# A written-out order of all steps, replaced by another: gated linear attention followed by a cosine-gated MLP

## The chip, the cores and the metric

The kernel runs on one core of one Trainium2 chip. The metric is the device time of one execution in microseconds; lower is better. Five engines work side by side, each through its own list of instructions in order: PE (TensorE, matmuls), ACT (ScalarE), DVE (VectorE), POOL (GpSimd), and SP (SyncE, which here only issues transfers).

## The reference

```python
# q, k, v, f_logit: 4 x 8 x 768 x 48 (batch, head, time, dim), float32
f = 1 / (1 + exp(-f_logit))
for t in range(768):
    state = f[:, :, t, :, None] * state + k_t (outer) v_t
    y[:, :, t] = q_t @ state
x = y as 3072 tokens x 384
h = x @ w_in                 # 384 -> 2048
out = (h * cos(h)) @ w_out   # 2048 -> 384
```

## The kernel before

The recurrence is computed in chunks. The 3072 tokens are twelve **pairs** `n` of two chunks (256 tokens), three pairs to a batch entry; within an entry the state goes from pair to pair. A pair is a set of named steps, most of them for the two halves `u` of the heads (suffix `.0`, `.1`):

- `f k q v` (SP, L309): loads. Pairs 0 and 1 fetch f, k and q by halves (192 KB each), everything else is 384 KB. `w0.i` and `w1.i` (L295, 768 KB) are the four parts of w_in and of w_out, `wc` their casts to bf16 (POOL or ACT, L196).
- `ex`, `ln` (ACT, L342, L346): softplus of the gate. `fx`, `fy`, `ka`, `qa`, `ad` (ACT and POOL, L350 to L373): the pairing of two neighbouring tokens in all pairs but 0 and 1.
- `cum` (PE, L386 and L392): running sums of the logarithms with the mask `incl`; `eb`, `ei` (ACT, L403, L407): their exponentials.
- `km`, `qm` (POOL, in pairs 0 and 1 also DVE, L416): k and q times those. `tk`, `tq` (PE, L451) transpose them in pairs 0 to 3 and `qkt` (L196) copies that out of PSUM; from pair 4 on `tq` is a transposing transfer on SP (L440).
- `sc` (PE, L472) scores, `am` (DVE, L494) their mask. `vb`, `vt` (POOL or ACT, L196) are copies of v.
- `ps` (PE, L512), `si` (PE, L529, pair 1 alone), `st`, `sz` (DVE, L538, L544): the state's sum, carry and decay.
- `y`, `yi` (PE, L572): the output inside the chunk and from the state; `xe` (ACT or DVE) copies it to bf16.

Behind a pair stands unit `m` of the MLP with the same 256 tokens: `h m.j s` (PE, L634, six matmuls, eight of these steps), `co` (ACT, cosine, L639), `g` (DVE, h times cosine, L616), and for each block of 128 tokens four steps `o` (PE, L650, four matmuls each), `ot` (copy) and `out` (store, L661). `z...` are memsets of padding (POOL or DVE, L241); `zf` (L277) is a matmul of zeros into a bank that nobody reads.

What runs when is one table, `ORDER`: every step once, with the letter of its engine (T PE, S ACT, V DVE, G POOL, Y SP) and the number of the buffer place that it takes. `emit` goes through it once and gives every engine its steps in this order; nothing is sorted afterwards. An instruction waits only for data, or for the place that its buffer frees.

Of the kernel before, what the change touches and what calls it, by code (L numbers as in the profile page):

```python
# [39 lines left out]
zsp.2:V zsz.0:V f1.0:Y ln1.1:S2 zvt.0:V zsp.1:V cum1.1:T2 k0.1:Y zf2:T3 q0.1:Y ei1.1:S0 vb0:G0  # L40
zf3:T1 ex0.1:S zf4:T4 f2:Y0 ex0.0:S vt0.2:G0 zf5:T6 ln0.0:S1 eb1.1:S0 cum0.0:T0 v1:Y1 ln0.1:S zf6:T5
zf7:T7 ei0.0:S1 zf8:T6 zf9:T6 cum0.1:T7 km0.0:G0 zf10:T4 f3:Y1 ei0.1:S zf11:T3 eb0.0:S1 zsz.3:G
tk0.0:T4 zf12:T6 eb0.1:S vt0.3:G km0.1:V ps0.0:T2,0 vt0.1:S k1.0:Y ex1.0:S ps0.1:T zf13:T6 sz0.00:V0
q1.1:Y0 vt0.0:S zf14:T6 zf15:T3 sz0.01:V zf16:T5 q1.0:Y st0.11:V zf17:T1 tk0.1:T6 ex2:S km1.1:V2
zf18:T1 w0.1:Y0 qm0.0:V tk1.1:T3 ln2:S1 zf19:T7 qm0.1:V tq0.0:T zf20:T5 vb1:S1 qkt0.0:V2 w0.0:Y3
ad2:G1 ln1.0:S sz0.11:V3 sc0.0:T4 tq0.1:T st0.10:V zsz.1:G ex3:S cum2:T2 am0.0:V1 w0.2:Y1 cum1.0:T7
vt1.1:G2 zf21:T1 ei1.0:S vt1.2:G zf22:T1 zf23:T1 ei2:S1 qkt0.1:V0 zf24:T4 km1.0:G zf25:T5 eb1.0:S
sz0.10:V ln3:S0 sc0.1:T6 ps1.1:T0,4 am0.1:V0 zf26:T1 eb2:S0 k3:Y2 ad3:G1 ps1.0:T fx3:S si1.0:T
tk1.0:T1 fx2:S qm1.0:V yi0:T5 qm1.1:G y0:T6 sz1.01:V1 tq1.0:T xe0.1:S2 cum3:T7 sz1.00:V w0.3:Y2
xe0.0:S qkt1.0:V0 tq1.1:T fy2:S zf27:T2 wc0.1:G qkt1.1:V1 eb3:S1 sc1.0:T0 ei3:S0 am1.0:V3 yi1:T3,2  # L50
vt1.0:S sc1.1:T6 q3:Y2 si1.1:T vt1.3:G am1.1:V0 h0.10:T0 wc0.0:S h0.11:T sz1.10:V1 sz1.11:V y1:T
w1.2:Y4 h0.01:T6 xe1.1:V0 wc0.2:G xe1.0:V h0.00:T co0.1:S3 k2:Y1 h1.01:T2 ka3:G h1.21:T4 fy3:S
g0.1:V0 co0.0:S2 h1.00:T km3.0:G2 h1.20:T w1.0:Y3 co1.0:S0 g0.0:V wc0.3:G h1.10:T0 co1.2:S3 h1.11:T
q2:Y1 g1.0:V1 qa3:G h0.30:T6 co1.1:S1 g1.2:V h0.31:T qm3.1:G h0.21:T2 co0.3:S2 g1.1:V km3.1:G
h0.20:T h1.31:T4 g0.3:V v3:Y2 qm3.0:G co0.2:S1 h1.30:T wc1.2:G tk3.0:T0 g0.2:V co1.3:S2 tq3.0:T
tq3.1:T6 w1.1:Y2 tk3.1:T qkt3.1:S2 ka2:G qkt3.0:V3 o2.2:T1 g1.3:V o1.2:T7 km2.1:G0 v2:Y1 o0.2:T0
wc1.0:S km2.0:G o3.2:T6 w1.3:Y4 sc3.0:T2 sc3.1:T4 qa2:G am3.0:V0 o0.0:T f4:Y2 o3.0:T qm2.1:G
am3.1:V2 vb3:S2 o2.0:T qm2.0:G tk2.1:T2 vt3.3:S0 tq2.1:T tk2.0:T3 qkt2.1:V4 f5:Y1 tq2.0:T ps3.0:T4,5
qkt2.0:V0 ps3.1:T wc1.1:G o1.0:T sz3.01:V0 sc2.0:T2 sz3.00:V k5:Y0 am2.0:V1 vb2:G0 o3.1:T o2.1:T
vt2.2:S2 vt3.1:G vt3.2:G ps2.1:T4 ps2.0:T sc2.1:T2 k4:Y2 st2.00:V wc1.3:G o0.1:T am2.1:V3 o1.1:T  # L60
st3.10:V v4:Y2 vt2.1:G o1.3:T ex4:S st3.11:V vt2.0:G o3.3:T ot1:V0 ln4:S1 vt2.3:G q4:Y1 o0.3:T
sz2.00:V3 ex5:S st2.01:V ad4:G2 o2.3:T sz2.01:V fx4:S ot3:V1 q5:Y2 ln5:S0 vt3.0:G cum4:T4 ot2:V2
y2:T2,3 ei4:S2 yi2:T ad5:G2 fy5:S yi3:T6 f9:Y0 y3:T1 xe2.0:V2 fx5:S ka4:G xe2.1:V fy4:S cum5:T7
sz3.10:V1 ei5:S0 h2.11:T2 sz3.11:V ka5:G out2:Y eb5:S2 xe3.1:V1 h2.10:T eb4:S0 xe3.0:V km4.1:G2
h2.21:T6 ot0:V3 v5:Y1 h2.01:T4 km4.0:G co2.1:S2 h2.00:T h3.21:T0 qa4:G co2.0:S3 g2.1:V1 h3.20:T
f6:Y2 qm4.0:G h2.20:T co3.2:S1 g2.0:V h2.31:T2 qm4.1:G co2.2:S0 h2.30:T g3.2:V3 vb4:G2 tq4.1:Y0
h3.11:T4 co2.3:S2 qa5:G g2.2:V h3.10:T h3.31:T0 vt4.2:S0 vt4.3:G f7:Y1 g2.3:V co3.1:S3 h3.30:T
vt4.0:G km5.1:G0 o5.1:T7 co3.3:S1 g3.1:V tq4.0:Y1 o4.0:T6 qm5.1:G o5.2:T g3.3:V q6:Y0 qm5.0:G
ps4.0:T4,5 sc4.1:T2 ps4.1:T o5.3:T st4.00:V ex6:S vb5:G0 tq5.1:Y4 st4.01:V o4.1:T sz4.01:V3 km5.0:G
ln6:S0 sz4.00:V o5.0:T out1:Y st4.11:V zsz.2:G fx6:S o6.3:T0 am4.1:V2 k6:Y2 ex7:S vt5.1:G2 o6.1:T  # L70
vt5.3:G tq5.0:Y3 ln7:S1 st4.10:V ps5.1:T1 ad6:G1 ps5.0:T sc4.0:T2 sz4.10:V2 o4.2:T am4.0:V3 fx7:S
zqk.1:G v6:Y2 o4.3:T vt4.1:S vt5.0:G ot5:S0 cum6:T4 sz4.11:V ad7:G2 ot4:S2 yi4:T2,3 st5.01:V ei6:S0
y4:T sz5.01:V1 eb6:S1 vt5.2:G sc5.1:T6 st5.00:V xe4.1:S2 xe4.0:V cum7:T5 o6.2:T out4:Y am5.1:V1
ka6:G ei7:S2 v7:Y0 eb7:S0 h4.00:T2 out3:Y km6.0:G0 sz5.00:V sc5.0:T4 k7:Y0 h4.01:T am5.0:V3 out0:Y
h3.00:T6 q7:Y1 co4.0:S2 vb6:G0 zvt.1:V y5:T1,4 km6.1:G yi5:T g4.0:V2 h3.01:T xe5.0:S3 fy6:S
ps6.1:T5,1 ps6.0:T xe5.1:S h4.31:T2 q8:Y2 qa6:G sz6.01:V3 co3.0:S2 sz6.00:V h4.30:T qm6.1:G h5.10:T4
g3.0:V co4.3:S3 h5.11:T vt6.1:G1 h4.21:T6 qm6.0:G g4.3:V co5.1:S0 h4.20:T ka7:G tq6.0:Y2 fy7:S
h4.10:T2 g5.1:V0 co4.2:S1 vb7:G2 h4.11:T k9:Y1 h5.21:T4 vt7.2:G0 g4.2:V co4.1:S2 h5.20:T km7.0:G1
tq6.1:Y4 o6.0:T vt6.2:S g4.1:V km7.1:G co5.2:S3 o9.2:T6 f8:Y2 vt6.0:G o9.3:T vt6.3:S g5.2:V qa7:G
# [693 lines left out]
```

## Time and profile before

| | us |
|---|---|
| three runs | 179.11, 179.11, 179.7; median 179.11 |
| the profiled execution, own time | 179.25 |
| its span on the core | 177.4 |
| DVE, ACT, POOL busy | 134.3, 128.9, 106.3 |

The span counts from the first recorded instruction to the last; 1.85 us of the execution's own time lie around it. Granted clock of TensorE over the span: 0.998. "Busy" means that at least one instruction of the engine was under way. In the views below "idle before" is how long the engine stood in front of an instruction, and the name behind the arrow is what ended it. Groups and timeline give first the line of the kernel, then the tile written and the tiles read.

### The profile page before, as it was taken

Reading aid. Unit: us, or ns where it says so; the run is one execution under the profiler, and the core shown is the slowest. Engines: PE = TensorE matmul, PEld = TensorE weight load, DVE = VectorE, ACT = ScalarE, POOL = GpSimd, SP = SyncE. Lnnn points to the kernel's source line nnn. Section 1 sums busy time; section 2 is a strip of 40 time slices with the busy share of each in tenths; the row PEclk is TensorE's granted clock in tenths of the full one; section 3 lists DMA queues with packets and bytes.
Section 4 is the critical chain, followed back from the end, with each engine's and each line's share of the span. In section 5 each row is a group of like instructions: output and inputs, shape, how many; then the busy total and the mean of one; then the engine's idle time right before and its main releaser. Section 6 shows DMA issues by size and latency. Waiting matters only on the chain.

```text
span 177.4 us, 5663 instructions
## 1 busy us (share of the span) xinstructions
PE 168.1 (95%) x2402; PEld 121.8 (69%) x2402; DVE 134.3 (76%) x201; ACT 128.9 (73%) x179; POOL 106.3 (60%) x134
## 2 busy tenths in 40 slices
...
GB/s 137 321 323 370 351 378 372 285 366 322 252 137 108 147 260 232 262 299 147 231 242 263 315 155 154 204 199 193 0 0 167 166 0 89 81 60 0 44 4 133
DMA packets 74394, 34.45 MB, mean 194 GB/s; under 512 B 67457, under 2 KB 72833, under 8 KB 74369
## 3 DMA queue, kind: packets, MB, share of 16 engines
...
q8 instruction: 19, 0.31, 0.8%
q14 instruction: 7, 0.05, 0.1%
...
## 4 chain that ended last, share of the span: by engine, by line
PE 85%; DVE 7%; POOL 3%; ACT 3%; issue 1%; POOLq 0%; DVEq 0%
PE ps L650 36%; PE ps L634 34%; PE ps L572 5%; PE ps L472 4%; PE ps L386 2%; PE ps L512 2%; DVE qk L416 2%; PE ps L451 1%; DVE qkt L196 1%; DVE incl L217 1%; ACT bj L403 1%; DVE sz L544 1%; PE ps L277 1%; DVE x L196 1%; DVE am L494 1%
## 5 line engine op out<-in xcount | busy, mean ns | idle before, releaser
L616 DVE TENSOR_TENSOR g<-ps,co 128x1024 bf16<-128x1024 f32 x48 | 57.8, 1222 | 15.4 <-ACT co L639 13.4
L650 PE MATMUL ps<-w_out_bf,g 128*128 128x384 bf16 x384 | 67.3, 326 | 0.0
L634 PE MATMUL ps<-x,w_in_bf 128*128 128x256 bf16 x576 | 66.3, 273 | 0.2 <-DVE x L196 0.2
L639 ACT ACTIVATE co<-ps,halfpi 128x1024 bf16<-128x1024 f32 x48 | 52.7, 1113 | 16.9 <-PE ps L634 13.0
L634 PEld LDWEIGHTS <-w_in_bf 128*128 128x128 bf16 x576 | 55.5, 98 | 8.5 <-issue 0.4
L650 PEld LDWEIGHTS <-g 128*128 128x128 bf16 x384 | 36.2, 98 | 22.4 <-DVE g L616 0.2
L494 DVE TENSOR_TENSOR am<-ps,pmask 128x1024 bf16<-128x1024 f32 x24 | 28.6, 1218 | 5.8 <-PE ps L472 4.5
L416 POOL TENSOR_TENSOR qk<-k,bi 128x384 bf16<-128x384 f32 x20 | 19.8, 1000 | 0.6
L416 POOL TENSOR_TENSOR qk<-q,b 128x384 bf16<-128x384 f32 x20 | 19.7, 999 | 0.7
L373 POOL TENSOR_TENSOR sp<-ls 128x384 bf16<-128x384 f32 x10 | 10.0, 998 | 13.3 <-ACT ls L346 7.1
L196 POOL COPY vt<-vb 64x384 bf16<-64x384 bf16 x32 | 16.0, 501 | 2.6 <-ACT vb L196 1.0
L196 ACT COPY ot<-ps 128x384 f32<-128x384 f32 (+1 forms) x10 | 4.5, 461 | 12.7 <-PE ps L650 6.9
L544 DVE TENSOR_TENSOR sz<-ps,b 64x192 bf16<-64x192 f32 x32 | 11.3, 354 | 1.3 <-PE ps L512 0.4
L196 DVE COPY ot<-ps 128x384 f32<-128x384 f32 (+1 forms) x16 | 8.1, 514 | 5.5 <-PE ps L650 5.5
L360 POOL TENSOR_TENSOR k<-k,f 128x384 f32<-128x384 f32 x10 | 10.0, 1002 | 3.4 <-ACT ot L196 3.3
L538 DVE TENSOR_TENSOR ps<-ps,sz 64x192 f32<-64x192 f32 x28 | 10.3, 366 | 1.8 <-PE ps L512 0.8
L342 ACT ACTIVATE f<-f 128x768 f32<-128x768 f32 (+1 forms) x14 | 10.3, 746 | 1.0 <-DMA f<-in_f_logit_dram 0.8
L277 PE MATMUL ps<-zero 128*128 128x512 bf16 x28 | 9.8, 445 | 1.2 <-DVE zero L203 1.2
L350 POOL TENSOR_TENSOR q<-f,q 128x384 f32<-128x384 f32 x10 | 10.0, 1000 | 1.3 <-ACT f L353 1.3
L196 ACT COPY vt<-vb 64x384 bf16<-64x384 bf16 x16 | 8.1, 508 | 2.4 <-POOL vb L196 2.1
L472 PE MATMUL ps<-qkt 48*64 48x128 bf16 (+1 forms) x320 | 8.8, 219 | 0.7 <-DVE qkt L196 0.6
L196 POOL CAST vb<-v 128x768 bf16<-128x768 f32 x8 | 6.6, 824 | 4.7 <-DMA v<-in_v_dram 3.4
...
## 6 DMA issues: line engine op xcount, KB each, us to landing
...
```

The source lines that it names most:

```text
L196: (nc.scalar.copy if e == "ACT" else eng(e).tensor_copy)(out=o, in_=i)
L277: G.step(f"zf{i}", ("PE",), lambda e, dump=dump: nc.tensor.matmul(dump.ap, lhsT=zero[:, 0:128], rhs=zero, start=True, stop=True), writes=[ ...
L342: nc.scalar.activation(out=flat(t.ap), in_=flat(t.ap), func=AF.Exp, scale=-1.0)
L416: G.step(f"{nm}{n}.{u}", ("POOL", "DVE") if cut else ("POOL",), lambda e, u=u, j=j, src=src, dec=dec: eng(e).tensor_mul(out=qkp[u][j].ap[: ...
L472: nc.tensor.matmul(o[t0:t1, r, 2 * a + g, :].rearrange("p (e n) -> p e n", e=2), lhsT=wide[s, t0 // 64, :] if turned else wide[s].rearrang ...
L494: G.step(f"am{n}.{u}", ("DVE",), lambda e, u=u, sc=sc: nc.vector.tensor_mul(out=am[u].ap.rearrange("p r b n -> p (r b) n"), in0=sc.ap.rear ...
L538: nc.vector.tensor_add(out=view()[s], in0=view()[s], in1=S0.ap[s, :, r, :])
L544: eng(e).tensor_mul(out=new.ap[s, :, r, :].rearrange("p (u a) n -> p u a n", u=2), in0=view()[s].rearrange("p (u a) n -> p u a n", u=2), i ...
L616: nc.vector.tensor_mul(out=o.rearrange("p b (n e) -> p b n e", e=2), in0=ph.ap.rearrange("p (b e n) -> p b n e", e=2, n=64), in1=co.ap.rea ...
L634: nc.tensor.matmul(ph.ap[:, i * T:(i + 1) * T].rearrange("p (g t) -> p g t", t=C), lhsT=w_in_bf[:, kk, f0:f0 + 128], rhs=xa[:, :, kk, :], ...
L639: G.step(f"co{m}.{j}", ("ACT",), lambda e, ph=ph, co=co: nc.scalar.activation(out=co.ap, in_=ph.ap, func=AF.Sin, bias=halfpi), reads=[ph], ...
L650: nc.tensor.matmul(po.ap[:, 0:DM], lhsT=gT.ap[:, j, i * C:(i + 1) * C], rhs=w_out_bf[:, j, :], start=(po.first and j == 4 * s), stop=(po.f ...
```

## The change

`ORDER` is another table, and `ZEROS`, the number of matmuls of zeros, goes from 28 to 21. No function changes. With one line fewer, each line number in the changed kernel is one lower (L309 is L308). The real steps are the same; most have another place in the order, many another buffer place, and some another engine: the first two loads go from ACT's queue to SP's, `vt0.0`, `vt0.1` and the cast `wc0.0` from ACT to POOL, `wc1.1` from POOL to ACT, `qkt0.0` and `qkt0.1` from DVE to ACT, `km0.0` from POOL to DVE.

```diff
-ZEROS = 28
+ZEROS = 21
...
-f1.1:Y2 f0.1:S1 zf0:T5 v0:Y0 f0.0:S zf1:T0 q0.0:Y1 zqk.2:G k1.1:Y1 zqk.0:G zvt.2:G k0.0:Y2 ex1.1:S
...
+f0.0:Y2 zf0:T5 v0:Y2 zf1:T7 k0.1:Y0 zsz.0:G zf2:T4 zsz.3:G f0.1:Y zvt.0:G f1.0:Y1 zsp.2:G k0.0:Y
...
```

Three places, as the built programs have them. SP's first transfers before; the number behind a tile's name tells its buffer place (`f_2` with 128x4x96 is half a pair's f), and two more halves of f stand at the head of ACT's list:

```order
L309 DMA f_2_97<-in_f_logit_dram 128x4x96
L309 DMA v_0_104<-in_v_dram 128x8x96
L309 DMA q_1_102<-in_q_dram 128x4x96
L309 DMA k_1_99<-in_k_dram 128x4x96
L309 DMA k_2_100<-in_k_dram 128x4x96
```

and in the changed kernel, where ACT's list has no load:

```order
L308 DMA f_2_97<-in_f_logit_dram 128x4x96
L308 DMA v_2_106<-in_v_dram 128x8x96
L308 DMA k_0_98<-in_k_dram 128x4x96
L308 DMA f_2_97<-in_f_logit_dram 128x4x96
L308 DMA f_1_96<-in_f_logit_dram 128x4x96
L308 DMA k_0_98<-in_k_dram 128x4x96
L308 DMA f_1_96<-in_f_logit_dram 128x4x96
```

Pair 0 now comes first (f, v, k), and pair 1's f stands fifth and seventh; before, the very first load was the second half of pair 1's f. Behind these the two orders reach the same point: the sixteenth half-or-whole load is followed by w0.1, w0.0 and w0.2 in both.

POOL at the program's start, before, from the last of the masks to the first use of v:

```order
masks.py:66 AFFINE_SELECT upper<-upper 128x128
L241 MEMSET qk_117 128x32x16
L241 MEMSET qk_115 128x32x16
L241 MEMSET vt_125 128x16x2x16
L196 CAST vb_118<-v_104 128x768
```

and in the changed kernel:

```order
masks.py:66 AFFINE_SELECT upper<-upper 128x128
L240 MEMSET sz_135 128x384
L240 MEMSET sz_138 128x384
L240 MEMSET vt_123 128x16x2x16
L240 MEMSET sp_109 128x16x16
L240 MEMSET qk_115 128x32x16
L240 MEMSET qk_117 128x32x16
L195 CAST vb_118<-v_106 128x768
```

Six memsets stand ahead of the first cast where there were three; DVE, which had four memsets behind its own masks, has one there now.

POOL ahead of the first weights (`w_in_bf<-g` is `wc0.1`), before:

```order
L373 TENSOR_TENSOR sp_108<-ls_111 128x8x48
L241 MEMSET sz_136 128x384
L196 COPY vt_125<-vb_119 64x8x48 x2
L416 TENSOR_TENSOR qk_117<-k_99,bj_121 128x8x48
L373 TENSOR_TENSOR sp_108<-ls_110 128x8x48
L416 TENSOR_TENSOR qk_117<-q_101,bb_161 128x8x48
L196 CAST w_in_bf<-g_143 128x3x512
```

and in the changed kernel:

```order
L415 TENSOR_TENSOR qk_117<-q_103,bb_162 128x8x48
L415 TENSOR_TENSOR qk_115<-q_101,bb_161 128x8x48
L195 CAST vb_118<-v_104 128x768
L195 COPY vt_125<-vb_118 64x8x48
L415 TENSOR_TENSOR qk_117<-k_100,bj_121 128x8x48
L415 TENSOR_TENSOR qk_117<-q_103,bb_162 128x8x48
L372 TENSOR_TENSOR sp_108<-ls_111 128x8x48
L372 TENSOR_TENSOR sp_109<-ls_110 128x8x48
L195 CAST w_in_bf<-g_147 128x3x512
```

`ad2` and `ad3` (the two `sp<-ls`) now stand together, right ahead of the first weights' cast, behind the products `qm1.1`, `qm0.1`, `km1.0` and `qm1.0`.

151 lines of the change are left out of this document (75 added, 76 removed).

## The prediction

> **What bounds the kernel now.** I read the page's list of engines first, then windows that I cut where PE's work changes. In a window's row stand the length and then the busy time of PE, PEld, DVE, ACT and POOL with the number of instructions.
>
> ```profile
> PE 168.1 (95%) x2402; PEld 121.8 (69%) x2402; DVE 134.3 (76%) x201; ACT 128.9 (73%) x179; POOL 106.3 (60%) x134
> ...
> 23.90:174.30 150.40, 149.99 (x2133) 111.24 (x2131) 119.11 (x163) 110.83 (x145) 92.78 (x109) 1.00 0.71 177
> 174.30:177.40 3.10, 0.00 (x0) 0.00 (x0) 0.00 (x0) 0.38 (x1) 0.00 (x0) 0.88 0.42 146
> ```
>
> From 23.9 us on PE is busy for 149.99 of 150.40 us: no other engine and no transfer bounds that stretch, it is PE's own list from end to end. The last 3.1 us are one copy and the last store. The matmuls of both kernels are the same (2402 less 28 of zeros is 2374, and so is 2395 less 21). So an order can do four things: begin the dense stretch earlier, move work across its beginning, open holes in it, or change the tail. I read its beginning next, in the timeline (start, length, engine, line, the idle time before in brackets).
>
> ```profile
> 18.36 0.86 ACT L346 ACTIVATE ls<-f 128x768 f32<-128x768 f32 x1
> 19.29 1.00 POOL L373 TENSOR_TENSOR sp<-ls 128x384 bf16<-128x384 f32 x1 [0.44 <-ACT ls L346]
> 20.18 0.55 DVE L416 TENSOR_TENSOR qk<-q,bb 128x384 bf16<-128x384 f32 x1
> 20.25 1.34 POOL L416 TENSOR_TENSOR qk<-q,bb 128x384 bf16<-128x384 f32 x1
> 21.54 1.46 POOL L196 CAST w_in_bf<-g 128x1536 bf16<-128x1536 f32 x1
> ...
> 22.82 0.52 PE L572 MATMUL ps<-qkt,sz 128*32 128x128 bf16 x24 [0.24 <-DVE qkt L196]
> 23.27 0.40 PE L472 MATMUL ps<-qkt 48*128 48x128 bf16 x8
> 23.95 1.47 PE L634 MATMUL ps<-x,w_in_bf 128*128 128x256 bf16 x12
> ```
>
> At 23.95 the first h step starts (`h0.10`), and it stands directly behind small matmuls of pair 1: PE's own list decides here. The cast of its weights had ended at 23.0, two copies of x long before. **The head**, the 23.95 us before, in which zeros fill many of PE's waits, is what the new order can shorten. Its start:
>
> ```profile
> 1.75 0.98 POOL L241 MEMSET qk<- 128x512 bf16 x2
> 1.84 1.39 DVE L217 COPY incl<-upper 64x64 bf16<-64x64 bf16 x1 [0.43 <-POOL upper masks.py:66]
> 2.68 0.53 POOL L241 MEMSET vt<- 128x512 bf16 x1
> 3.64 0.18 DVE L217 COPY incl<-upper 64x64 bf16<-64x64 bf16 x1
> 3.96 0.52 ACT L342 ACTIVATE f<-f 128x384 f32<-128x384 f32 x1 [0.80 <-DMA f<-in_f_logit_dram]
> 4.30 0.17 DVE L241 MEMSET sp<- 128x128 uint32 x1
> 4.51 0.52 ACT L346 ACTIVATE sp<-f 128x384 bf16<-128x384 f32 x1
> 5.08 0.32 PE L386 MATMUL ps<-sp,incl 128*128 128x192 bf16 x1 [2.87 <-DVE sp L241]
> 6.01 0.49 ACT L403 ACTIVATE bj<-ps 128x384 f32<-128x384 f32 x1 [0.97 <-PE ps L392]
> 6.20 0.82 POOL L196 CAST vb<-v 128x768 bf16<-128x768 f32 x1 [3.00 <-DMA v<-in_v_dram]
> ...
> 15.79 0.40 PE L472 MATMUL ps<-qkt 48*128 48x128 bf16 x8 [0.58 <-DVE qkt L196]
> ```
>
> The first half of f is there at 3.95 (ACT stood for it), the first v at 6.2 (POOL stood for it). PE's first real matmul waits 2.87 us, and the releaser is DVE's memset, not ACT, whose `ln` was done at 5.03: the masks come first.
>
> **The change part by part.** I follow the new list engine by engine to `h0.10`, with durations of before. Transfers first:
>
> ```profile
> 3.00:14.00 11.00, 8.37 (x81) 4.71 (x81) 4.24 (x19) 7.76 (x17) 3.38 (x6) 1.00 1.17 322
> 15.50:24.00 8.50, 7.74 (x178) 5.21 (x179) 7.95 (x14) 7.42 (x17) 7.43 (x10) 1.00 1.03 371
> ```
>
> The 16 DMA engines are full (share 1.17 and 1.03) at 322 GB/s while halves of 192 KB (196,608 bytes) arrive, so 0.61 us each; the weights come at 371 GB/s, 2.1 us for 768 KB. The loads keep coming one behind the other, so what lands when is a count of units: the first at 3.9 (estimate, as before; one queue instead of two may change it by some tenths either way), each unit 0.6 later. New landings by that: `f0.1` 6.3, `k0.0` 7.5, `f1.1` 8.1, `q0.0` 9.9, `f2` 11.1, `v1` 12.9, `f3` 14.7, `q1.0` 15.3, then `w0.1` 17.4. Twenty units stand ahead of the weights in both orders, so the end of this row does not move; what moves is who comes first in it.
>
> *Masks.* DVE's 64x64 copy took 1.39 us at 1.84 and 0.18 at 3.64. The first ended at 3.23, POOL's three memsets beside it at 3.21. I take it that the copy stood until POOL's run was over. POOL's run is now six memsets: two of sz, one of vt, one of sp, two of qk.
>
> ```profile
> L241 POOL MEMSET sz<- 128x384 bf16 x3 | 1.2, 416 | 0.0
> ```
>
> 0.42 each for sz, 0.53 for vt and 0.98 for the two of qk stand above; that of sp, 256 columns, isn't there and lies between 0.20 (128 columns) and 0.42 (384), I take 0.3. With 0.05 of overlap each the run ends at about 4.3 instead of 3.2. From DVE's release to its first memset of sp 1.2 us passed (3.24 to 4.46), so `cum0.0` starts at 5.5 where the first sum started at 5.08. Three memsets fewer on DVE (0.6) are already in this.
> The Trainium skill, "SBUF — State Buffer", section "Who interferes with whom", says that DVE and GpSimd share one pair of ports under an exclusive lock, taken by a copy in a two-port mode, and the later one blocks until the other's instruction is over. The trace agrees (1.39 against 0.18), though there two further memsets passed before the copy got through. If the copy doesn't stand, the masks are ready long before 5.0, and `cum0.0` follows `ln` there: 0.5 earlier.
>
> *ACT until the sums of pair 1.* The table is loaded before the first f lands, and ACT then stood for it (0.80 idle at 3.96), so the two issues that it loses cost nothing. Rows:
>
> ```profile
> L342 ACT ACTIVATE f<-f 128x768 f32<-128x768 f32 x10 | 8.4, 838 | 0.1
> L196 ACT COPY qkt<-ps 128x1024 bf16<-128x1024 bf16 x1 | 1.0, 1003 | 0.0
> ...
> 17.61 0.48 ACT L407 ACTIVATE bi<-ps 128x384 f32<-128x384 f32 x1
> 17.98 0.50 ACT L403 ACTIVATE bb<-ps 128x388 f32<-128x388 f32 x1
> ```
>
> In a run the next starts 0.1 before the last one's end (17.61 and 0.48 against 17.98), so I count 0.1 less: 0.42 for a half of `ex` or `ln`, 0.74 for a whole one, 0.39 for `ei` and `eb`, 0.9 for `qkt`. From `cum0.0` at 5.5 (0.93 to its exponential, as 5.08 to 6.01): `ei0.0` to 6.9, then `ex0.1`, `ln0.1`, `eb0.0`, `ex1.0`, `ex1.1`, `ln1.1` to 9.6. `cum1.1` could start there, but PE's list has six zero matmuls and `ps0.0` ahead of it, behind `cum0.1`.
>
> ```profile
> 5.83 1.87 PE L277 MATMUL ps<-zero 128*128 128x512 bf16 x4
> 8.67 1.38 PE L277 MATMUL ps<-zero 128*128 128x512 bf16 x4
> 12.11 1.25 PE L277 MATMUL ps<-zero 128*128 128x512 bf16 x5
> ```
>
> Four zeros took 1.87 at first, five took 1.25 later: 0.47 against 0.25 each; the four of 8.67 lie between (1.38), so the rate changes in their middle, near 9.4. So: four zeros to 8.1, `cum0.1` to 8.8, three zeros at 0.45 and three at 0.22 to 10.8, `ps0.0` 0.3, `cum1.1` 0.4, and `eb1.1` starts at about 11.4. This is the first place where zeros stand in the way, and the price is in the sum. From there ACT's list is full: `eb1.1`, `ln1.0`, `ei1.1`, `ex2`, `qkt0.0`, `ei1.0`, `eb1.0`, `qkt0.1`, `ex3`, `ln2`, `ln3`: 4 x 0.39 + 0.42 + 4 x 0.74 + 2 x 0.9 + 0.1 = 6.8 us, to 18.2, and I add 0.3 for two short waits on transposes. `f3` has landed by then.
>
> *POOL to the weights.* `ad2` waits for `ln2` (17.7), so `ad2`, `ad3` at 0.95 each and `wc0.1` at 1.46 end at 21.1. `w0.1` is there at 17.4. POOL's products before that (`qm1.1` from 11.9, `qm0.1`, `vb1`, `vt1.3`, `km1.0`, `qm1.0`) end at about 17.2, hidden by the wait for `ln2`.
>
> *DVE and PE beside it.*
>
> ```profile
> 20.76 0.72 DVE L544 TENSOR_TENSOR sz<-ps,bb 64x192 bf16<-64x192 f32 x2
> 21.41 1.36 DVE L196 COPY qkt<-ps 128x1024 bf16<-128x1024 bf16 x2
> 22.69 2.35 DVE L494 TENSOR_TENSOR am<-ps,pmask 128x1024 bf16<-128x1024 f32 x2
> ```
>
> DVE runs full from `km1.1` (12.9, behind `ei1.1`) to the mask `am1.1`: one product at 0.5, seven of `sz` and `st` at 0.36, two `qkt` at 0.68, three masks at 1.17, 7.9 us, to 20.8 with its overlaps. The place that it reads is the one that `sc1.0` writes, the last step ahead of `h0.10` (0.35): 21.1. So two chains end at **21.1**: 2.85 us before the 23.95 of now.
>
> *Across the border.* `yi1` (0.45 by the rows at 22.82 and 23.27 of the same stretch, 24 matmuls) now stands behind `h0.10`: +0.45. All other real steps ahead of `h0.10` are the same. Inside, the groups of h, o and small steps alternate a little differently; a first o or h step behind small ones costs up to 0.1 more, and a handful of such changes either way is bounded by -0.5 and +0.5; I take 0.
>
> *Dense stretch and tail.* No zeros stand there in either list. Every other move is worth nothing while PE stays full: POOL, with some eight more instructions, is busy for 92.78 of those 150.40. The last step is `o20.1` instead of `o21.0`, with the same copy and store: 0.
>
> Sum: 179.25 - 2.85 + 0.45 = 176.85; the profiled execution lies 0.14 above the median. Predicted: **176.8 us**.
>
> **The rivals.**
>
> *The plan doesn't hold: holes in the dense stretch.* PE comes 2.85 earlier, ACT less so: behind the copies of x (20.4) stand seven small steps, 2.9 us, and a table load before the first cosine.
>
> ```profile
> 24.83 1.28 ACT L639 ACT_TABLE_LOAD   x1
> L639 ACT ACTIVATE co<-ps,halfpi 128x1024 bf16<-128x1024 f32 x48 | 52.7, 1113 | 16.9 <-PE ps L634 13.0
> L616 DVE TENSOR_TENSOR g<-ps,co 128x1024 bf16<-128x1024 f32 x48 | 57.8, 1222 | 15.4 <-ACT co L639 13.4
> 25.98 9.28 PE ps L634 x84
> ```
>
> So `co0.1` starts at 24.7 and `g0.1` ends at 27.0. An h step takes 0.66 (9.28 for 14), and `h1.10`, which needs that PSUM place, comes at 21.1 + 1.4 + 0.45 + 0.55 + 6 x 0.66 = 27.4. The margin is 0.4; later it grows, since ACT and DVE need 1.0 and 1.15 where PE needs 1.3. For it: margins this thin exist at several places (the casts of w_out on ACT and POOL have 0.5 to 1.3). Against: the list before was as tight and left 0.4 idle in 150. A hole of 1.0: **177.8**.
>
> *DVE shut out by POOL.* `km1.1` (two inputs in SBUF) falls into POOL's run from `qm1.1` to `vb1`. At 20.18 DVE's product began while POOL worked and took its normal 0.55; POOL's next one took 1.34 instead of 1.00. So the price is between 0 and, if DVE has to sit out the run as at 1.84, 2 us for `tk1.1`, `cum1.0` and all behind. I take 0, the nearer row (the same instruction). At 2: head to 23.1, **178.9**, no change that can be told.
>
> *The masks don't stand.* If DVE's 1.39 had another cause and the first f, alone on its queue, lands at 3.5, then the head ends 0.9 earlier, DVE's chain bounding it: **175.9**.
>
> *The clock, the slower side.* Zeros go from 28 to 21 while the head keeps its waits. Say PE falls back to the early rate (0.47 for a zero) between 11 and 21 and reaches `h0.10` with it. The small matmuls between the links of the chain (some 2 us, an estimate) would take twice as long, and the dense stretch would run at half rate until the rate returns; that took from 5.08 to 9.4, 4.3 us, at a loss of 2.2. 176.85 + 4.2 = **181.0**. It decides from the point where the holes in PE's list last long enough; the longest now, 0.6 us ahead of 15.8, did nothing, and the new list has holes of the same size by my count.
> The Trainium skill, "TensorE: Matmul & The Clock Gate", section "What's actually happening", has the clock fall after an idle window of about 3.4 us and rise after a busy one, with windows that run freely. The trace's rise after 4.3 us fits; no run here shows a fall.
>
> **How the numbers follow.** Forecast (176.0 to 177.4) 0.53; holes 0.16; DVE shut out 0.13; masks free 0.10; clock 0.08. The range takes in all but the last, and the two at its ends by half, with their own spread of some 0.5: 175.7 to 178.9. A measurement of this kernel tells about 0.5% (0.9 us) from no change: faster means below 178.2, which holds for forecast, masks and most of the holes: 0.77; within: 0.14; slower: 0.09.
>
> **What would show it.** Right: the first L633 matmul near 21.1; `cum0.0` near 5.5, behind a DVE copy of over 2 us; `wc0.1` ending within 0.2 of `h0.10`; PE over 99% busy from there on. Wrong: idle PE of over a microsecond behind `h0.10`, with L615 or L195 as the releaser; a DVE L415 of over 1 us near 13; zeros at 0.45 behind 12.

## The result, and the profile after

| | before | changed |
|---|---|---|
| median of 20 runs each, us | 179.66 (178.74 to 180.30) | 177.87 (176.47 to 180.49) |
| ratio, 95% interval | | 0.9897 [0.9871, 0.9922] |
| profiled execution: own time, span | 179.25, 177.4 | 177.66, 175.9 |
| first h step (`h0.10`) starts | 23.95 | 21.41 |

The change makes the kernel 1.0% faster, some 1.85 us (0.0103 x 179.66). The forecast was 176.8; the median lies 1.07 above it and inside the range of 175.7 to 178.9. The ratios here and below leave out executions more than 1.5% above their kernel's fastest (four of the 20 of the changed kernel, none of those before), while the medians keep them; the changed kernel scatters more, and the two medians alone give 0.9900.

The page's engines and the two windows that answer to those of before, the first from `h0.10` to PE's end (length, then the busy time of PE, PEld, DVE, ACT, POOL):

```profile
PE 166.0 (94%) x2394; PEld 120.8 (69%) x2395; DVE 129.1 (73%) x187; ACT 131.2 (75%) x185; POOL 110.6 (63%) x142
...
21.40:172.70 151.30, 150.03 (x2156) 112.00 (x2156) 114.36 (x153) 114.50 (x156) 94.95 (x113) 1.00 0.74 185
172.70:175.90 3.20, 0.00 (x0) 0.00 (x0) 0.00 (x0) 0.48 (x1) 0.00 (x0) 0.89 0.19 71
```

The row of before (23.90 to 174.30: 149.99 busy of 150.40) ends 0.13 behind PE's last matmul, this one 0.04. Counted from `h0.10` to that last matmul the stretch is 150.22 long with 0.26 idle before (23.95 to 174.17), and 151.25 long with 1.22 idle now (21.41 to 172.66); the tail is 3.2 in both. The ledger adds up: the dense stretch begins 2.54 earlier, PE is busy in it 0.07 longer and idle 0.96 longer, which makes -1.51, and the span lost 1.50. So the head came nearly as forecast, and more than a third of it was given back in idle time of PE. That is in one place; PE's timeline there, and POOL's and SP's ahead of it (SPq is SP's queue, the length that of the issue):

```profile
72.80 0.49 PE L633 MATMUL ps<-x,w_in_bf 128*128 128x256 bf16 x3
73.79 0.31 PE L511 MATMUL ps<-vb,qk 64*64 64x48 bf16 x16 [0.50 <-POOL vb L195]
74.75 0.31 PE L511 MATMUL ps<-vb,qk 64*64 64x48 bf16 x16 [0.65 <-POOL qk L415]
...
66.17 2.06 POOL L195 COPY vt<-vb 64x384 bf16<-64x384 bf16 x4
70.88 1.00 POOL L359 TENSOR_TENSOR k<-k,f 128x384 f32<-128x384 f32 x1 [2.66 <-DMA k<-in_k_dram]
71.96 1.01 POOL L415 TENSOR_TENSOR qk<-k,bi 128x384 bf16<-128x384 f32 x1
72.91 0.83 POOL L195 CAST vb<-v 128x768 bf16<-128x768 f32 x1
73.69 1.00 POOL L415 TENSOR_TENSOR qk<-k,bi 128x384 bf16<-128x384 f32 x1
...
58.86 2.61 SPq L439 DMA_TRANSPOSE qkt<-qk  x1
61.52 0.58 SPq L308 DMA_DIRECT2D v<-in_v_dram  x1
62.19 4.44 SPq L439 DMA_TRANSPOSE qkt<-qk  x2
66.68 0.58 SPq L308 DMA_DIRECT2D k<-in_k_dram  x1
```

Read it from the top: `ps6.1` and `ps6.0` wait 1.15 us for POOL. POOL had stood 2.66 us ahead of `ka6` for the load `k6`. SP issued `k6` at 66.68, behind three transposing transfers whose issues take up to 3 us each; the two that stand together took 4.44.

### The profile page after: what moved, and what is told of

It is laid out like the page before. It is cut to its first block, busy times and chain, and to the rows that moved or that the text cites. A ratio compares the mean times of both kernels' runs of the same rounds, so it can differ in the third digit from the quotient of the medians.

```text
span 175.9 us, 5652 instructions
## 1 busy us (share of the span) xinstructions
PE 166.0 (94%) x2394; PEld 120.8 (69%) x2395; DVE 129.1 (73%) x187; ACT 131.2 (75%) x185; POOL 110.6 (63%) x142
## 4 chain that ended last, share of the span: by engine, by line
PE 63%; DMA 16%; POOL 9%; SPq 5%; ACT 3%; issue 3%; POOLq 0%
PE ps L633 28%; PE ps L649 27%; DMA g<-in_moe_w_in_dram 6%; DMA g<-in_moe_w_out_dram 5%; SPq L308 5%; PE ps L571 4%; POOL qk L415 3%; DMA v<-in_v_dram 3%; DMA k<-in_k_dram 2%; PE ps L471 2%; POOL w_out_bf L195 2%; POOL sp L372 1%; POOL k L359 1%; PE ps L511 1%; POOL vb L195 1%
## 5 line engine op out<-in xcount | busy, mean ns | idle before, releaser
L615 DVE TENSOR_TENSOR g<-ps,co 128x1024 bf16<-128x1024 f32 x48 | 57.1, 1220 | 16.2 <-ACT co L638 13.3
L638 ACT ACTIVATE co<-ps,halfpi 128x1024 bf16<-128x1024 f32 x48 | 52.1, 1114 | 15.4 <-PE ps L633 12.6
L195 POOL COPY vt<-vb 64x384 bf16<-64x384 bf16 x36 | 18.2, 508 | 1.9
L195 ACT COPY ot<-ps 128x384 f32<-128x384 f32 (+1 forms) x15 | 6.8, 451 | 13.1 <-PE ps L649 12.5
L195 ACT CAST x<-ps 128x384 bf16<-128x384 f32 x15 | 6.9, 478 | 5.0 <-PE ps L571 5.0
L195 DVE COPY ot<-ps 128x384 f32<-128x384 f32 (+1 forms) x11 | 5.6, 515 | 4.9 <-PE ps L649 4.8
L471 PEld LDWEIGHTS <-qkt 48*64 48x64 bf16 (+1 forms) x320 | 5.9, 104 | 4.2 <-issue 3.2
L345 ACT ACTIVATE ls<-f 128x768 f32<-128x768 f32 x10 | 8.3, 838 | 0.2
```

Of the source, the lines that this page charges most:

```text
L195: (nc.scalar.copy if e == "ACT" else eng(e).tensor_copy)(out=o, in_=i)
L471: nc.tensor.matmul(o[t0:t1, r, 2 * a + g, :].rearrange("p (e n) -> p e n", e=2), lhsT=wide[s, t0 // 64, :] if turned else wide[s].rearrang ...
L615: nc.vector.tensor_mul(out=o.rearrange("p b (n e) -> p b n e", e=2), in0=ph.ap.rearrange("p (b e n) -> p b n e", e=2, n=64), in1=co.ap.rea ...
L638: G.step(f"co{m}.{j}", ("ACT",), lambda e, ph=ph, co=co: nc.scalar.activation(out=co.ap, in_=ph.ap, func=AF.Sin, bias=halfpi), reads=[ph], ...
```

## The experiments

In all of them only `ORDER` is edited (in e4 `ZEROS` too). "Idle" is PE's idle time from the wait ahead of `h0.10` to its end, in gaps over 0.05 us, from the trace of the profiled execution; ratios are to the kernel before on the same chip, from 5 to 20 executions of each version. Single executions of one kernel differ by 2 us and more, so mechanisms are read from the traces and sizes from the ratios.

| | `h0.10` | idle | PE ends | own time | median | ratio, 95% |
|---|---|---|---|---|---|---|
| before | 23.95 | 0.26 | 174.17 | 179.25 | 179.66 | 1 |
| changed | 21.41 | 1.38 | 172.66 | 177.66 | 177.87 | 0.9897 [0.9871, 0.9922] |
| e9_head_alone_c | 21.23 | 0.30 | 171.73 | 177.15 | 178.03 | 0.9917 [0.9887, 0.9946] |
| e3_head_alone | 22.47 | 1.13 | 174.20 | 179.46 | 179.40 | 0.9982 [0.9954, 1.0010] |
| e6_head_alone_b | 22.62 | 1.22 | 175.50 | 181.08 | 179.56 | 1.0043 [1.0010, 1.0076] |
| e5_rest_alone | 24.00 | 0.90 | 174.72 | 180.15 | 178.95 | 0.9963 [0.9930, 0.9995] |
| e1_k6_early | 21.85 | 1.77 | 173.83 | 178.81 | 178.61 | 0.9919 [0.9886, 0.9952] |
| e7_k6_v6 | 20.84 | 0.59 | 171.57 | 176.55 | 176.55 | 0.9846 [0.9797, 0.9894] |
| e2_masks_free | 21.66 | 1.26 | 172.74 | 178.05 | 178.02 | 0.9886 [0.9843, 0.9930] |
| e8_q1_first | 20.85 | 1.18 | 172.01 | 177.30 | 177.62 | 0.9900 [0.9869, 0.9931] |
| e4_no_zeros | 21.78 | 1.20 | 173.01 | 177.99 | 177.17 | 0.9886 [0.9844, 0.9928] |
| e10_both | 22.73 | 0.00 | 172.45 | 177.49 | 177.01 | 0.9862 [0.9825, 0.9898] |
| e11_both_w13 | 21.61 | 1.35 | 173.36 | 178.35 | 177.29 | 0.9861 [0.9817, 0.9905] |
| e12_two_queues | 21.98 | 1.95 | 174.30 | 179.27 | 177.40 | 0.9852 [0.9815, 0.9889] |

### The hole ahead of ps6: e1_k6_early, e7_k6_v6

```diff
 v7:Y2
+k6:Y1
 ... tq4.0:Y0 ... v6:Y1 ... tq5.1:Y4 ... tq5.0:Y2
-k6:Y1
 v8:Y0
```

> The changed kernel with one step moved: the load k6 stands ahead of the transposing transfer tq4.0 on SP instead of behind tq5.0. Theory (PE's 1.14 us of idle time ahead of ps6.1 and ps6.0 come from k6's late issue, and nothing else is late behind it): k6 is issued near 59 and lands before 65, POOL's 2.66 us of idle time ahead of ka6 go, ps6.1 and ps6.0 follow h3.01 without a gap, the profiled time falls by 1.0 to 1.2 us to about 176.5, ratio to the kernel before 0.983 to 0.985. Rival 1 (the transfers are one queue, so what is moved ahead delays tq4.0, v6 and tq5.x): sc4.0 or sc5.x get late instead, PE idles about as long there, time 177.4 to 178. Rival 2 (POOL's own work is what is late): ka6 comes earlier, the gap at ps6 stays over 0.6.

`k6` landed at 65.18, `ka6` came at 69.9 and the gap at `ps6` was gone, but PE had a new one. Its timeline in e1:

```profile
63.72 2.44 PE L649 MATMUL ps<-w_out_bf,g 128*128 128x384 bf16 x14
67.69 0.42 PE L471 MATMUL ps<-qkt 48*64 48x128 bf16 x16 [1.52 <-DMA qkt<-qk]
```

`sc4.0` now waits 1.52 for `tq4.0`, the transposing transfer that `k6` was put in front of. Rival 1 holds: SP's queue is one line, the transfer behind `k6` was urgent too, and pushing ahead costs whoever is pushed back. So the next run exchanges two loads and delays no transposing transfer:

```diff
 tq4.0:Y0
-v6:Y1
+k6:Y1
 tq5.1:Y4 ... tq5.0:Y2
-k6:Y1
+v6:Y1
```

> The changed kernel with two loads of SP exchanged: k6 stands where v6 stood (between the transposing transfers tq4.0 and tq5.1), v6 where k6 stood (behind tq5.0). No transposing transfer has more ahead of it than in the changed kernel. Theory (the hole ahead of ps6 is k6's place, and the sc4.0 hole of e1 was the price of pushing tq4.0 back): k6 lands near 66.5, ka6 starts near 68.3, v6 lands near 70.7 and vb6 follows at 70.7 to 71.6, ps6.1 and ps6.0 have no idle time over 0.1 ahead of them, sc4.0 neither; profiled time 1.0 to 1.2 below the changed kernel's, 176.5; ratio to the kernel before 0.982 to 0.985. Rival 1 (vb6, now last, is late instead): idle PE of 0.5 to 1.1 at ps6 remains. Rival 2 (the slack of the transfers is used up and another one is late): a new hole of over 0.5 elsewhere, time about 177.5.

POOL and PE in e7, at the same place:

```profile
67.77 1.00 POOL L359 TENSOR_TENSOR k<-k,f 128x384 f32<-128x384 f32 x1
68.85 1.00 POOL L415 TENSOR_TENSOR qk<-k,bi 128x384 bf16<-128x384 f32 x1
70.04 0.82 POOL L195 CAST vb<-v 128x768 bf16<-128x768 f32 x1 [0.19 <-DMA v<-in_v_dram]
...
72.84 0.44 PE L511 MATMUL ps<-vb,qk 64*64 64x48 bf16 x32
```

`ka6` follows POOL's copies without a wait, `vb6` waits 0.19 for its load, and both `ps6` steps run behind the h step with no gap. The own time is 1.11 below the changed kernel's, as the theory had it, but not by its sum: the hole's 1.15 went and the head ended 0.57 earlier in this execution, but 0.34 was given back at 89 us, where `y6` now waits for a bank that a copy on ACT frees, and PE was busy 0.17 longer:

```profile
89.73 0.41 PE L571 MATMUL ps<-am,vt 128*32 128x128 bf16 x16 [0.34 <-ACT ot L195]
```

The ratio, 0.9846 from five executions, is 0.5% below the changed kernel's, with intervals that overlap: that the hole is gone is shown by the trace, what it is worth over many executions is not. The hole is not in every execution: e4 and e8 leave `k6` where it was and have no gap at `ps6`. There the two transposing transfers that stand together took 3.45 and 3.08 instead of 4.44, so SP issued `k6` at 65.09 and 65.07 instead of 66.68 and `ka6` started 0.8 and 1.0 earlier, while PE came to `ps6.1` 1.7 and 0.5 later (at 74.97 and 73.76, where the changed kernel's PE was free at 73.29).

### The two halves of the change: e3, e6, e9, e5

Both tables do the same steps ahead of certain points, so one's head can be joined to the other's rest; only buffer places are renamed.

```diff
 (changed table up to h0.10)
+h0.10:T0 wc0.0:S h0.11:T ...   (the old rest)
```

> The first 140 steps of the changed table (up to h0.10), then the remaining steps in the order and on the engines of the kernel before (eb3, ei2, ei3, fx2 and yi1, which the old table has ahead of h0.10, come first; buffer places renamed to fit). It is the head's part of the change alone. Theory (the head's 2.54 us reach the end, since the old rest had no holes and PE's list is full): yi1 stands ahead of h0.10 again, so h0.10 starts near 21.9, PE idles under 0.6 us behind it, profiled time 179.25 - 2.1 = 177.2 (176.9 to 177.5). Rival (the old rest cannot start earlier: its loads, casts or cosines are late for a PE that comes 2 us sooner): h0.10 near 21.9, but 1 us or more of idle PE behind it, time 178 to 179.

The time did not move, and neither reason expected is the whole of it. PE in e3, and windows of it (the number behind the five engines is the granted clock):

```profile
21.00 0.52 PE L571 MATMUL ps<-qkt,sz 128*32 128x128 bf16 x24
22.47 2.51 PE L633 MATMUL ps<-x,w_in_bf 128*128 128x256 bf16 x12 [0.96 <-DVE am L493]
...
19.10:22.50 3.40, 1.80 (x51) 1.23 (x46) 2.88 (x4) 3.26 (x9) 2.09 (x3) 1.00 1.05 374
22.70:26.10 3.40, 3.40 (x46) 2.24 (x44) 0.37 (x2) 3.37 (x4) 2.73 (x3) 0.50 1.10 369
```

The old rest writes `h0.10` into a bank that the new head's last mask still reads: 0.96 us of waiting. Twelve matmuls of h then take 2.51 instead of the 1.47 of before, because for 3.4 us the granted clock is 0.50. The steps behind `h0.10` became 1.51 us longer than before, which is all that the head had gained in this execution (23.95 - 22.47 = 1.48). The forecast's rival of a falling clock is this mechanism, met by another door. But the slow clock is not the whole reason for the ratio: only four of the twelve executions have a mean granted clock of 0.987 to 0.990, which is one such stretch, and the other eight have 0.997 to 1.000. The four took 180.13 us on average, the eight 179.15, against 179.79 before: a price of 1.0, and without it still only 0.6 of gain. The wait for the bank is the candidate for what is left; no trace of those eight shows it. e6 renames the banks:

> As e3_head_alone (the changed head, then the rest in the old order), with one thing else: the banks of the rest are named so that h0.10 writes the pair of banks that it writes in the changed kernel, and not the one that am1.0 still reads. Theory (in e3 the mask am1.0 held h0.10's bank for 0.96 us, and PE, idle so long in a stretch where it was half busy anyway, was put to half clock for 3.4 us): h0.10 starts within 0.2 of the end of yi1, near 21.7 + (landing of q1.0 - 16.9), the granted clock stays at 1.00 from 9 us on, PE ends near 172.1 to 172.5, time 177.0 to 177.5, ratio 0.985 to 0.989. Rival 1 (the clock falls for another reason, such as the fewer zeros): it falls here too, time 178.5 to 179.5. Rival 2 (the old rest cannot use an earlier start): over 1 us of idle PE behind h0.10, time 178 or more.

It missed too: `h0.10` was free, but the renaming put `yi1` ahead of it into the bank of `ei2`; PE waited 0.77 there, and the clock was 0.50 from 22.89 to 26.30. Six of the eleven executions have a mean clock of 0.988 to 0.990 (180.07 on average, the other five 179.25, and 179.03 before, so without the slow clock e6 still gains nothing). e9 cuts behind `yi1` instead:

```diff
 (changed table up to yi1)
+y1:T w1.2:Y3 h0.01:T2 ...   (the old rest)
```

> The head alone once more, cut at another place: the changed table up to y1 (150 steps, yi1 behind h0.10 as in the changed kernel), then the rest in the old order; at this cut both tables have done the same steps, and no bank of the first matmuls behind the cut is one that a head's step still reads. Theory (in e3 and e6 the head was as early as in the changed kernel, and what ate it was a wait of PE of 0.8 to 1.0 us right at h0.10 and the half clock behind it): h0.10 starts 4.5 behind q1.0's landing (21.0 to 21.8), the granted clock stays at 1.00, PE's list from there is 150.2 + 0.4 for yi1 long, PE ends near 172.0, time 177.0 (176.6 to 177.6), ratio 0.983 to 0.989: the head is worth about 2.1 us by itself. Rival (the old rest cannot use an earlier start): over 1 us of idle PE behind h0.10 and a time of 178 or more.

```profile
21.20:171.80 150.60, 150.23 (x2160) 111.58 (x2156) 119.20 (x162) 111.81 (x150) 94.82 (x111) 1.00 0.72 184
```

The head alone: 2.7 earlier, 0.30 idle behind `h0.10`, clock 1.00 throughout (0.997 or more in all seven executions), own time 2.10 below the profiled execution of before; by the ratio 1.5 us (0.0083 x 179.69). PE's busy time is 0.24 longer than the 149.99 of before; `yi1`, now inside, is the step that was added. The other half:

```diff
 (old table up to h0.10)
+h0.10:T0 wc0.0:G h0.11:T ...   (the changed rest)
```

> The kernel before up to h0.10 (with its 28 zeros), then the remaining steps as the changed table has them (yi1, eb3, ei2, ei3 and fx2 stay ahead of h0.10; buffer places renamed to fit). It is the rest's part of the change alone. Theory 1 (the hole ahead of ps6 belongs to SP's list and comes with the new rest wherever the head ends): h0.10 near 23.95, 0.8 to 1.2 us of idle PE ahead of ps6.1 and ps6.0, regrouping -0.5, time 179.25 - 0.5 + 1.1 = 179.8. Theory 2 (the hole opens only because PE comes 2.5 us earlier, while transfers and POOL do not): no idle PE there, time 179.25 - 0.5 = 178.7. In both the sum of this run's and the head-alone run's differences from 179.25 is that of the changed kernel (-1.6) only if the parts add up; under theory 2 they would sum to -2.6.

```profile
23.95:174.75 150.80, 149.86 (x2133) 111.62 (x2131) 114.69 (x153) 112.82 (x150) 94.07 (x112) 1.00 0.72 179
174.75:178.40 3.65, 0.00 (x0) 0.00 (x0) 0.00 (x0) 0.48 (x1) 0.00 (x0) 0.78 0.17 63
```

PE waits 0.17 and 0.64 ahead of `ps6.1` and `ps6.0` though it comes two microseconds later: theory 1, the hole belongs to the new rest. This execution is the second longest of the kernel's twelve (178.11 to 180.20); the ratio says that the rest is worth -0.4% all the same. This trace cannot explain that gain: its own ledger is a loss (0.64 more in gaps, 0.45 more behind PE's end, 0.13 less busy). Whether the hole is missing in the shorter executions, as it is in e4 and e8, no trace shows. The halves multiply to 0.9917 x 0.9963 = 0.9880, against 0.9897 for the whole: they add up within their intervals. In e10, which has the changed rest with `k6` and `v6` exchanged and no hole, PE is busy for 149.75 us, `yi1` included, against e9's 150.23 with the old rest; in the changed kernel it is 150.03. So regrouping is worth between 0.2 and 0.5 by these single profiles (0.13 by e5's 149.86 against the 149.99 of before, both without `yi1`).

### What sets the head's end: e2, e8, e4, e12

```diff
-k0.1:Y0 zsz.0:G zf2:T4 zsz.3:G f0.1:Y zvt.0:G f1.0:Y1 zsp.2:G k0.0:Y zqk.0:G zqk.2:G f1.1:Y ... vb0:G0
+k0.1:Y0 zf2:T4 f0.1:Y f1.0:Y1 k0.0:Y f1.1:Y ... vb0:G0 zvt.0:G zqk.0:G zsp.2:G
...
-vt0.1:G
+vt0.1:G zqk.2:G zsz.0:G zsz.3:G
```

> The changed kernel with POOL's six memsets ahead of vb0 moved behind it (zvt.0, zqk.0, zsp.2) and behind vt0.1 (zqk.2, zsz.0, zsz.3), so that POOL does nothing while DVE makes the masks. Theory A (DVE's 64x64 copy of 2.37 us stood for POOL's memsets, but the masks are not on the path, since ex0.1 waits for f0.1's landing at 6.4 whatever cum0.0 does): the copy takes about 0.2, cum0.0 starts near 4.7 or when ln0.0 ends, h0.10 stays within 0.3 of 21.4, time as the changed kernel (177.7, within 0.4). Theory B (as the prediction had it: the masks cost what they delay cum0.0): h0.10 comes 0.3 to 0.5 earlier, time about 177.2. Theory C (the copy's length has nothing to do with POOL): the copy still takes over 1.3.

DVE's first mask copy in the changed kernel with POOL's memsets beside it, and then the same copy in e2:

```profile
1.86 2.37 DVE L216 COPY incl<-upper 64x64 bf16<-64x64 bf16 x1 [0.44 <-POOL upper masks.py:66]
1.76 0.77 POOL L240 MEMSET sz<- 128x384 bf16 x2
2.48 0.53 POOL L240 MEMSET vt<- 128x512 bf16 x1
2.94 0.31 POOL L240 MEMSET sp<- 128x256 bf16 x1
3.20 0.99 POOL L240 MEMSET qk<- 128x512 bf16 x2
```

```profile
1.85 0.17 DVE L216 COPY incl<-upper 64x64 bf16<-64x64 bf16 x1 [0.44 <-POOL upper masks.py:66]
```

2.37 us with POOL's six memsets, 0.17 without: the blocking is shown. It cost nothing: `cum0.0` started at 4.66 instead of 4.87, and ACT's `ex0.1` waited for `f0.1` in both (6.26 behind a landing at 6.24, 6.43 behind 6.41). `h0.10` came at 21.66, time and ratio are the changed kernel's. Theory A.

The Trainium skill, "SBUF — State Buffer", section "Who interferes with whom", has the lock held for one instruction of the other engine. The trace agrees that DVE stands, and shows more: 2.37 us over six instructions, the longest of which is 0.53.

```diff
-f3:Y2 ... q1.0:Y
+q1.0:Y f3:Y2
...
-ex3:S ... ln2:S1
+ln2:S1 ex3:S
```

> The changed kernel with q1.0 loaded ahead of f3 instead of behind it, and ln2 ahead of ex3 on ACT, since f3 comes later. Theory (in the changed kernel's head POOL's qm1.0, ad2, ad3, wc0.1 follow q1.0's landing, and h0.10 comes 4.5 behind that landing: 16.89 and 21.41, 17.35 and 21.85, 17.16 and 21.66 in three profiles): q1.0 lands near 15.7, qm1.0 starts when km1.0 ends (16.4), wc0.1 ends near 20.8, h0.10 starts at 20.8 to 21.2, bounded by DVE's am1.1 and sc1.0; gain 0.3 to 0.6, time about 177.2. Rival (as the prediction had it: ACT's ln2 and ln3 set the head, f3 matters): f3 lands near 16.9, ln3 ends near 18.6, ad3 and wc0.1 are not earlier, h0.10 at 21.4 or later.

The changed kernel's POOL first, then e8's:

```profile
17.03 1.01 POOL L415 TENSOR_TENSOR qk<-q,bb 128x384 bf16<-128x384 f32 x1 [0.60 <-DMA q<-in_q_dram]
17.98 1.96 POOL L372 TENSOR_TENSOR sp<-ls 128x384 bf16<-128x384 f32 x2
19.88 1.48 POOL L195 CAST w_in_bf<-g 128x1536 bf16<-128x1536 f32 x1
```

```profile
15.98 0.99 POOL L415 TENSOR_TENSOR qk<-q,bb 128x384 bf16<-128x384 f32 x1
16.94 2.06 POOL L372 TENSOR_TENSOR sp<-ls 128x384 bf16<-128x384 f32 x2
18.95 1.46 POOL L195 CAST w_in_bf<-g 128x1536 bf16<-128x1536 f32 x1
```

In the changed kernel `qm1.0` waits 0.60 for `q1.0` (landed at 16.89), and the two `ad` and the cast follow without a gap to 21.35. In e8 the load came at 13.94, no wait is left, the cast ends at 20.41, and `h0.10` follows `sc1.0` instead, at 20.85. The time did not follow, since PE then waited at the next bound, the last quarter of w_out (POOL and PE in e8):

```profile
44.01 1.46 POOL L195 CAST w_out_bf<-g 128x1536 bf16<-128x1536 f32 x1 [1.73 <-DMA g<-in_moe_w_out_dram]
45.53 1.79 PE L649 MATMUL ps<-w_out_bf,g 128*128 128x384 bf16 x10 [1.18 <-POOL w_out_bf L195]
```

In the changed kernel the same cast ends at 44.94 and `o2.3` starts at 44.99, behind 0.08 of idle time: the slack is used up there already.

All but three traces with the new head fit one rule, within 0.03 us. `h0.10` starts at the later of two times: `q1.0`'s landing + 4.5 (changed 16.89 and 21.41, e1 17.35 and 21.85, e2 17.16 and 21.66, e7 16.32 and 20.84), and `eb1.1`'s start + 10.15 (e8 10.70 and 20.85, e9 11.07 and 21.23, e11 11.46 and 21.61, e12 11.82 and 21.98, e10 12.58 and 22.73). Three traces lie outside it: e3 and e6 with their banks, and e4, where `w0.1` landed at 20.20. The first time was stated before e8 and e9 ran, and e9, forecast by it, came 0.74 later (15.99 + 4.5 = 20.49 against 21.23); the second was read off afterwards, and no run was made to test it. It moves by 2 us with PE's rate. The six zeros ahead of `cum1.1`, and `eb1.1` behind it, in the changed kernel and then in e10:

```profile
8.17 1.46 PE L276 MATMUL ps<-zero 128*128 128x512 bf16 x6
10.42 0.49 ACT L402 ACTIVATE bb<-ps 128x388 f32<-128x388 f32 x1 [0.33 <-PE ps L391]
```

```profile
8.76 2.72 PE L276 MATMUL ps<-zero 128*128 128x512 bf16 x6
12.58 0.49 ACT L402 ACTIVATE bb<-ps 128x388 f32<-128x388 f32 x1 [2.12 <-PE ps L391]
```

Same list, same place: 1.46 with the rate up at 8.2, 2.72 with the rate still low, and ACT idle for 2.12 where it had 0.33. Would it be better without zeros?

```diff
-zf0:T5 ... zf20:T1
-ZEROS = 21
+ZEROS = 0
```

> The changed kernel without any of its 21 matmuls of zeros; everything else stands as it was. Theory A (the zeros hold the clock up: without them PE is busy for less than half of the head): the granted clock is 0.5 in most of the head or falls back to it, small matmuls take twice as long, h0.10 comes 0.5 to 2 later, and the first 3 us of the dense stretch run at 0.5, at a loss of about 1.7; time 179.5 to 182. Theory B (the clock rises anyway, and the zeros only stand in the way of cum1.1): eb1.1 starts 0.2 to 0.3 earlier, h0.10 at 21.2 to 21.4, time 177.3 to 177.7.

Neither theory alone. `eb1.1` came at 10.40, as early as in the best run with zeros. The full rate came late, as theory A has it: four transposes took 0.59 at 13.71 us in e4 and 0.40 at the same place in the changed kernel, and the trace's clock record has the rise at 14.79 instead of 7.97. Then PE was busy for only 1.27 us of the 3.4 ahead of `h0.10`, waited 1.20 for `wc0.1`, and the clock was 0.50 for the next 3.35:

```profile
18.40:21.80 3.40, 1.27 (x21) 0.92 (x22) 2.88 (x4) 3.36 (x9) 2.25 (x3) 0.97 1.06 368
21.70:25.05 3.35, 3.27 (x36) 2.25 (x40) 0.85 (x3) 2.63 (x5) 3.08 (x4) 0.50 1.10 360
```

In this execution PE was busy for 151.23 us behind `h0.10` instead of 150.03 and began 0.37 later, but the hole at `ps6` did not open, which saves 1.22 of idle time; the ratio is 0.9886, the changed kernel's within the intervals. A table without the six zeros ahead of `cum1.1` but with the fifteen others was not tried.

```diff
-f0.0:Y2 zf0:T5 ... f0.1:Y
+f0.0:S2 f0.1:S zf0:T5 ...
```

> The changed kernel with the two halves of pair 0's f loaded from ACT's queue, as the kernel before has its first two loads; SP's list then starts with v0. Theory A (one queue instead of two keeps the 16 DMA engines less full: 296 to 318 GB/s from 3 to 14 us in seven profiles with the new head, 319 and 322 in the two with the old one): 318 to 325 GB/s in that stretch, q1.0 lands near 16.1, h0.10 starts near 20.7, time 0.3 to 0.7 below the changed kernel's. Theory B (the rate varies from run to run and has nothing to do with the queue): the rate lies between 296 and 318, q1.0 lands at 16.1 to 17.3, h0.10 at 20.8 to 21.8. Besides, f0.1 lands with f0.0 near 3.9, ahead of v0 and k0.1, so ei0.0 and ex0.1 start by 5.8 and vb0 later, near 6.0; neither was on the path.

The stretch of the halves, in the changed kernel and then in e12 (the last number is GB/s):

```profile
3.00:14.00 11.00, 8.51 (x100) 5.11 (x101) 6.99 (x19) 8.61 (x18) 6.75 (x13) 1.00 1.12 305
```

```profile
3.00:14.00 11.00, 7.27 (x85) 4.54 (x86) 5.24 (x17) 7.36 (x17) 6.37 (x12) 1.00 1.16 320
```

With two queues the rate was 320 and `q1.0` landed at 15.48. But the first half of f came at 5.07 instead of 3.49, `cum0.0` at 6.22, and `h0.10` at 21.98 by the other chain. The three profiles with loads on two queues have 319 to 322 GB/s, the eleven with one have 296 to 318. That leans to theory A and doesn't settle it: e6, e8 and e11 reach 318 with one queue. This profiled execution is its kernel's longest of six (176.18 to 179.27), so its time says little.

### Together: e10_both, e11_both_w13

e10 has the edits of e7 and e8. e11 has a third one beside them:

```diff
-f4:Y2 ... w1.3:Y4
+w1.3:Y4 f4:Y2
...
-ad4:G1 ... vt2.3:G vt2.2:G
+vt2.3:G vt2.2:G ad4:G1
```

> The edits of e7 and e8 together: k6 and v6 exchanged, q1.0 ahead of f3, ln2 ahead of ex3. Theory (behind the head the next bound is the weights: in every run with the new rest o2.3 starts within 0.1 us of the end of the cast wc1.3, which starts as w1.3 lands at 42.8 to 43.9, so a head that ends earlier only waits there): h0.10 near 20.8, 0.5 to 1.2 us of idle PE ahead of o2.3, no idle PE at ps6, time as e7 alone within 0.4 (176.3 to 176.9). Rival (the gains add up): PE idle under 0.2 everywhere, PE ends near 170.9, time 175.9 or less.

> As e10_both, and the load w1.3 stands ahead of f4 on SP instead of behind it (384 KB less ahead of it, 1.2 us by the rate of that stretch); on POOL vt2.3 and vt2.2 go ahead of ad4, since f4 and so ln4 come later. Theory (w1.3's landing holds o2.3): w1.3 lands 1.2 earlier than in e10, near 42, wc1.3 ends near 43.7, o2.3 has no idle time ahead of it; cum4 and y2 behind it have at most 0.3; PE ends 0.4 to 1.0 earlier than in e10, time 175.6 to 176.1. Rival (f4 is as urgent as w1.3): cum4 waits for ad4 by as much as o2.3 gains, time as e10.

In e10 the question could not be put: the clock rose late, `h0.10` came at 22.73, and at `o2.3` the cast had been done for 1.1 us. It shows what the changed rest, with `k6` exchanged, does when nothing is late: not one gap over 0.05 us behind `h0.10`. In e11 `w1.3` landed at 41.30 and `o2.3` did not wait, but `y3` did, 0.71 for `vt3.3` on ACT, which stood behind `ln5` and so behind `f4`, landed at 43.69. That is the rival: `f4` is as urgent as `w1.3`. Two more waits, 0.23 and 0.35, stood at 91 us. The 175.9 that adding up would give is a ratio of 0.979, below both intervals: the gains did not add up.

## Why the forecast was right, and where not

- **What bounds the kernel, and the sign.** Right. PE's list was full, an earlier head reached the end, and e9 shows the head by itself: 2.1 us in the profile, 1.5 by the ratio.
- **The head's size.** 21.1 said, 21.41 measured, 20.8 to 22.7 over all traces of that head. That it is only 0.3 off is in part luck, since another chain than the forecast's set it (next point). The step "the loads keep coming one behind the other" took 322 GB/s for the new list; it had 305 up to 14 us. `q1.0` landed at 16.89 and not 15.3, `w0.1` at 18.76 and not 17.4; "the end of this row does not move" was off by 1.3.
- **Who ends last in the head.** The forecast had POOL waiting for `ln2` at 17.7. In the profiled execution `ln2` was done at 17.25 and POOL's list, called "hidden by the wait for `ln2`", was what counted, through `q1.0`. The chain of ACT and DVE that the forecast drew, by the rule above, would have given 10.42 + 10.15 = 20.57 here; it decides in e8 to e12, where `q1.0` came earlier or `eb1.1` later. Its term "`eb1.1` starts at about 11.4" is in the middle of what the runs have, 10.40 to 12.58; when the full rate comes draws the lot. DVE's chain was forecast to end with `am1.1` at 20.8, and did so at 20.80, by luck: `km1.1` began at 11.74 and not 12.9, and the chain took 9.1 and not 7.9.
- **Masks.** The mechanism was right, and shown by e2; that the delay stands on the path was wrong. `cum0.0` was at 4.87 instead of 5.5, and behind it `ex0.1` waits for `f0.1` anyway. The rival "masks don't stand" falls with it: e2 took the stall away and the head did not move, although the first f landed early, at 3.49, as that rival had it.
- **`yi1`.** 0.45 said, 0.24 by e9 if nothing else in its dense stretch changed.
- **Regrouping, taken as 0 within 0.5.** It brought 0.1 to 0.5 by the profiles, inside the bound and on its good side.
- **Holes.** This rival happened, at about its price (0.96 against 1.0) and beside the forecast instead of in place of it. The place named, `h1.10` behind `g0.1`, showed no wait. The step of the sum that failed is "every other move is worth nothing while PE stays full": I weighed POOL's and ACT's lists against PE's and did not walk SP's list through the dense stretch, where loads stand behind transposing transfers: `k6` was issued at 66.68 and PE stood 1.15 us for it. The thin margins of the w_out casts were named rightly: 0.08 of idle time in the changed kernel, 1.18 in e8.
- **DVE shut out.** `km1.1` took 0.73 instead of 0.56, between POOL's products: the nearer row was the better guide.
- **The clock.** It did not fall ahead of PE's end in any of the 20 executions of the changed kernel (0.997 or more); in the traces of e3, e4 and e6 it fell. The point from which it decides was set too far off ("the longest now, 0.6 us ahead of 15.8, did nothing"): waits of 0.77, 0.96 and 1.20 us just ahead of `h0.10` were enough. Its price was too high: 1.5 in e3's trace, not 4.2.
- **The signs.** They point both ways: PE was busy for 99.2% of the dense stretch (150.03 of 151.30), as said for a right forecast, and it idled for over a microsecond behind `h0.10` with L195 among the releasers, as said for a wrong one.

The sum, by the ledger: -2.54 for -2.85, +0.24 for +0.45, about -0.17 from regrouping and +0.96 of idle time, both taken as nothing: -1.51 for -2.40.
